# Two 32-head attentions on one core: unread matrix products in slots short of work, and a reordered start and end

## The chip, the cores and the metric

The kernel runs on one core of a Trainium2 chip. The metric is the device time of one execution in microseconds (us), smaller is better; it is the median of several executions. The engines are TensorE (PE in the profile, its weight loads PEld), VectorE (DVE), ScalarE (ACT), GpSimd (POOL) and SyncE (SP). They run at the same time, each through its own queue in order, and wait for each other by semaphores.

## The reference

Two attention blocks of the same shape, A over all keys and B over a sliding window, are computed from separate inputs and laid side by side in the output. x is 2048 x 512, wqkv 512 x 1536, wo 512 x 512, all bf16.

```python
def attention(x, wqkv, wo, window=None):        # B=1, S=2048, D=512, H=32, Dh=16
    q, k, v = split_heads(x @ wqkv)
    scores = einsum("bhqd,bhkd->bhqk", q, k) * Dh ** -0.5
    if window:                                  # block B: window = 256
        d = idx[:, None] - idx[None, :]
        scores = where((d >= 0) & (d < window), scores, -1e9)
    p = softmax(scores, axis=-1)
    return merge_heads(einsum("bhqk,bhkd->bhqd", p, v)) @ wo
out = concatenate([attention(A_x, A_wqkv, A_wo), attention(B_x, B_wqkv, B_wo, 256)], -1)
```

The great mass of the work is the exponential: for A alone 32 x 2048 x 2048 elements. With heads only 16 wide the matrix products have little to multiply per element of the scores.

## The kernel before

**Units, jobs, slots.** A unit is one block, one pass of 512 queries and one group of four heads. Its jobs are score tiles of 128 keys by 512 queries for one head. Three jobs make a slot (`SLOT = 3`): one PSUM tile `sps` of three banks, of which there are two. `slots` (L796) writes all jobs into one list of 755 slots, with B's units spread between A's. The four heads of a group use row groups 32j of the array, so that their score products run beside each other (L517); the products of probabilities and values use column groups 32j in the same way (L621).

**One turn of the loop.** `run` (L905) writes out the order of every engine's queue by hand. For slot s it issues the exponential of slot s on ScalarE (`exps`, L544), perhaps one step of a vector-side exponential (`dq`), the score products of slot s+2 (`scores`), the value products whose probabilities are ready (`values`), the transfers and small steps that are due (`later`), and then as many filling steps as a credit allows (`fill`, L889). Since there are two `sps` tiles, the scores of slot s+2 wait until the exponential of slot s has read its tile.

**Filling steps.** Projections of q, k and v, output products, and the score products of the jobs whose exponential VectorE computes as a polynomial (L571 to L595) are tasks with a due slot (`plan`, L819). Most are pairs: the first step opens PSUM bank `ms` (there is one) and does half the products, the second does the other half and empties the bank. While a pair is open, `self.open` holds the bank. `queued` and `freed` keep an estimate of when VectorE will have emptied it, in units of `PITCH` = 1.345 us a slot.

**The filler that is there.** In `scores`, where fewer than two steps were filled in the slot before and the job is A's, a product of 128 rows and 512 columns (L512) goes into the same `sps` bank first; the real score product then overwrites it.

**Sums and division.** Values carry a column of ones, so that each unit's bank `op` (one) also gets the softmax denominators. `epilogue` copies `op` to `osb` (L675) and sends it through DRAM; the denominators are gathered, inverted, spread and multiplied in four later steps (L681 to L703). Only the last two units of A's last pass divide in place (`end`, L641): a reciprocal of the whole bank (L649), ScalarE's copy (L651), four fp32 products that spread the reciprocals over rows (L655), and one multiply (L658). `last_out` (L402) then makes A's last output tile from five products for each of four query chunks and writes it out.

**Start.** `start` (L709) turns the tokens of A chunk by chunk (`turn`), copies them to SBUF (`keep`), makes the keys of the first two head groups with padding (`keys`, L443), the first queries, two value tiles, and the guard row that keeps exponents in range (`pad_guard`: L465, L467, L470, L472). `more_constants` sets up masks and fills eight DRAM scratch tensors `kd` and `qd` by GpSimd's queue.

Of the kernel before, what the change touches and what calls it, by code (L numbers as in the profile page):

```python
# [14 lines left out]
P = 128  # L15
H = 32
# [87 lines left out]
class _Kernel:  # L104

    def __init__(self, ctx, tc, tensors, out):
        self.tc, self.nc = tc, tc.nc
        self.t = tensors
        self.out = out
        pool = lambda name, **kw: ctx.enter_context(tc.tile_pool(name=name, **kw))  # L110
        self.consts = pool("consts", bufs=1)
        self.sb = pool("sb", bufs=1)
        self.ps = pool("ps", bufs=1, space=bass.MemoryType.PSUM)
        self.dram = pool("dram", bufs=1, space=bass.MemoryType.DRAM)
        self.xT, self.w, self.wo, self.kT, self.v, self.qT = {}, {}, {}, {}, {}, {}
        self.acol, self.negas, self.oT = {}, {}, {}
        self.op, self.od = {}, {}
        self.later = []
        self.slot = self.ended = self.closed = -1
        self.pend, self.guards, self.dq = [], [], []  # L120
        self.open = None
        self.filled = 2
        self.vec = self.freed = 0.0
        self.last_poly = -1
# [6 lines left out]

    def queued(self, us, bank=False):

        self.vec = max(self.vec, self.slot * PITCH) + us
        if bank:
            self.freed = self.vec


    def constants(self):
# [5 lines left out]
        pick(self.ident[:], self.ident[:], pattern=[[1, P]], compare_op=ALU.is_equal,  # L145
             fill=0.0, base=0, channel_multiplier=-1)
        self.wpad = self.tile([P, 2, NC, 2, P], BF16, "wo", 2)
        nc.gpsimd.memset(self.wpad[:].bitcast(FP32), 0.0)
# [169 lines left out]
    def v_evac(self, i, t, bank, copy, h=(0, H)):  # L318
        if i == 1:
            self.v_begin(i, t)  # L320
        v3 = self.v[i, t][:, 0:H * VP].rearrange("p (h d) -> p h d", d=VP)
        self.queued(OP, True)
        copy(out=v3[:, h[0]:h[1], 1:VP],
             in_=bank[:, 0:(h[1] - h[0]) * DH].rearrange("p (h d) -> p h d", d=DH))
# [77 lines left out]
    def last_out(self, i, p):  # L402

        nc = self.nc
        o, wo = self.oT[i, p], self.wo[i]
        big = [self.ps.tile([P, SLOT, 512], FP32, name="sps", tag="sps", bufs=2)
               for _ in range(2)]
        banks = [big[qc % 2][:, qc // 2, :] for qc in range(4)]

        def mm(qc, c):  # L410
            w = wo[:, c, :] if c < NC - 1 else self.wend[:, c - NC + 1, :]
            nc.tensor.matmul(banks[qc], lhsT=o[c][:, qc * P:(qc + 1) * P], rhs=w,  # L412
                             start=(c == 0), stop=(c == NC))
        for qc in range(4):
            for c in range(NC):
                mm(qc, c)

        def finish():
            obs = self.tile([P, SLOT, 512], BF16, "pT", 6)
            for qc in range(4):  # L420
                mm(qc, NC)
            for qc in range(4):
                ob = obs[:, qc, :] if qc < SLOT else self.tile([P, D], BF16, "ob", 2)[:]
                (nc.scalar.copy if qc % 2 else nc.vector.tensor_copy)(out=ob, in_=banks[qc])
                q0 = p * 512 + qc * P
                (nc.scalar if qc % 2 else nc.sync).dma_start(
                    self.out[q0:q0 + P, i * D:(i + 1) * D], ob)
        return finish

# [72 lines left out]
    def scores(self, slot):  # L502
        sps = self.ps.tile([P, SLOT, 512], FP32, name="sps", tag="sps", bufs=2)
        for b, jb in enumerate(slot["jobs"]):
# [4 lines left out]
            if b == 0 and self.filled < 2 and jb.inst == 0:  # L509

                kT, k0 = self.kT[jb.inst, jb.g // 2, jb.subs[0][0] // 4]
                self.nc.tensor.matmul(sps[:, 0, 0:WARM], lhsT=kT[:, gg, k0:k0 + P],  # L512
                                      rhs=qT[:, gg, 0:WARM], start=True, stop=True)
# [89 lines left out]
    def values(self):  # L603


        while self.pend:
# [4 lines left out]
            if key not in self.op:  # L611
                if self.ended >= self.slot - 1:
                    return
                self.op[key] = self.ps.tile([P, 512], FP32, name="op", tag="op", bufs=1)
                self.started = set()
            op = self.op[key]
            self.pend.pop(0)
            for jb in group:
                h = 4 * jb.g + jb.j
# [21 lines left out]
    def end(self, i, p, g):  # L641


        nc = self.nc
        op = self.op[i, p, g]
        ones = self.tile([P, 32], FP32, "den", 2)
        nc.gpsimd.memset(ones[:], 1.0)
        rec = self.tile([P, 512], FP32, "oc", 2)
        nc.vector.reciprocal(out=rec[:], in_=op[:])  # L649
        osb = self.tile([P, 512], FP32, "osb", 2)  # L650
        nc.scalar.copy(out=osb[:], in_=op[:])  # L651
        b = self.bank()
        for j in range(GH):
            r = slice(32 * j, 32 * j + 1)
            nc.tensor.matmul(b[32 * j:32 * j + 32, :], lhsT=ones[r, :], rhs=rec[r, :],  # L655
                             start=True, stop=True, tile_position=(32 * j, 32 * j))
        o = self.tile([P, 512], BF16, "oTa", 5)
        nc.vector.tensor_mul(out=o[:], in0=osb[:], in1=b[:])  # L658
        self.closed = self.slot
        self.queued(2.2, True)  # L660
        self.oT.setdefault((i, p), []).append(o)

    def epilogue(self, i, p, g):
# [11 lines left out]
        nc.vector.tensor_copy(out=osb[:], in_=self.op[i, p, g][:])  # L675
        self.queued(OP)
        nc.sync.dma_start(od[g % 2], osb[:])
        if g % 2 == 0:
# [11 lines left out]
        def invert():  # L690
            den = st["den"]
            nc.vector.reciprocal(out=den[:], in_=den[:])
            self.queued(0.35)
            st["rd"] = self.dram.tile([8, 512], FP32, name="rd", tag="rd", bufs=3)
# [6 lines left out]
        def scale():  # L701
            o = self.tile([P, 512], BF16, "oT" + n, 5)
            nc.vector.tensor_mul(out=o[:], in0=st["oc"][:], in1=st["rb"][:])  # L703
            self.queued(OP)
            self.oT.setdefault((i, p), []).append(o)
# [3 lines left out]
    def start(self):  # L709
# [28 lines left out]

        def busy(n):

            b = self.bank()
            for _ in range(n):
                nc.tensor.matmul(b[:, 0:P], lhsT=self.ident[:], rhs=self.ident[:],
                                 start=True, stop=True)

        def turn(c):
# [17 lines left out]
        def keys(c):  # L764
            b = tile_("op", 1) if c % 2 == 0 else self.bank()
            self.pad_mm(1, 0, c, b[:], range(NC))
            self.pad_k_evac(0, c, b[:])
        for t in range(NKT):
            self.v_begin(0, t)
        busy(36)  # L770
        turn(0)
        keep(0)
        turn(1)
        keys(0)
        keep(1)
        b = self.bank()
        self.pad_mm(0, 0, 0, b[:], range(NC))
        mq = self.pad_q_evac(0, b[:])
        for c in range(2, NPASS):
            turn(c)  # L780
            keys(c - 1)
            keep(c)
        keys(NPASS - 1)
        nv = 2
        for t in range(nv):
            vb = tile_("op", 1)
            self.v_mm(0, t, vb[:], range(NC), (0, HV))
            self.v_evac(0, t, vb[:], nc.scalar.copy, (0, HV))
            if t == 0:
                self.pad_guard(0, mq)  # L790
                self.qT[0, 0, 0] = self.padq
        self.more_constants()
        self.load_wo(0)
        return [("v", 0, t, 0) for t in range(nv)] + [("k", 0, 0), ("q", 0, 0, 0)]
# [24 lines left out]
    def plan(self, slots, done):  # L819
# [24 lines left out]
        for t in range(NKT):  # L844
            task(("v", 0, t, 0), vneed[0, t] - 1, self.v_steps(0, t, (0, HV)))
            task(("v", 0, t, 1), begin[0, 0, 2] - 16 + t, self.v_steps(0, t, (HV, H)),
                 [("v", 0, t, 0)])
# [41 lines left out]
    def fill(self, s, tasks, done):  # L889

        if self.open is None:
            if self.closed == s or self.freed > (s + 0.5) * PITCH:
                return False
# [11 lines left out]
    def run(self):  # L905
        done = set(self.start())
        self.vec = self.freed = 0.0
        slots, self.pend = self.slots()
# [4 lines left out]
        for s, sl in enumerate(slots):  # L913
            self.slot = s
            self.exps(sl)
            if self.dq and self.vec <= (s + 0.4) * PITCH:
                self.queued(1.22)
                self.dq.pop(0)()
            if s + 2 < len(slots):
                self.scores(slots[s + 2])  # L920
            self.values()
            due = [x for x in self.later if x[0] <= s]
# [10 lines left out]
            if (self.guards and self.guards[0][0] <= s and self.open is None  # L933
                    and self.freed <= (s + 0.5) * PITCH):
                self.guards.pop(0)[1]()
                self.closed = s
            while credit >= 1.0 and self.fill(s, tasks, done):
                credit -= 1.0
                self.filled += 1
        finish = self.last_out(0, NPASS - 1)  # L940
        while self.pend:
# [55 lines left out]
```

## Time and profile before

| | |
|---|---|
| time, median of three | 1124.56 us (1121.5 to 1127.27) |
| span of the profiled execution | 1120.5 us |
| ScalarE busy | 1033.3 us, 92% |
| TensorE busy | 974.3 us, 87% |
| VectorE busy | 636.4 us, 57% |
| GpSimd busy | 20.4 us, 2% |
| mean granted TensorE clock | 0.927 |
| chain that ended last | ACT 48%, PE 34%, issue 10%, DVE 7% |

The busy share of TensorE is that of its instructions' durations, which get longer when its clock is lowered; a busy TensorE is therefore not one at its peak. The clock line of the page gives the granted share of the full clock in tenths for each fortieth of the span (28 us). The chain is followed back from the last instruction to what released each one, and says which engine held up the end.

### The profile page before, as it was taken

The page shows a single profiled execution, that of the slowest core. Times are in us where ns is not written, and L with a number is a line of the kernel's source. Part 1 is how long each engine was busy: PE and PEld are TensorE (multiplying, and loading weights), DVE is VectorE, ACT ScalarE, POOL GpSimd, SP SyncE. Part 2 cuts the span into 40 slices and gives each one's busy share as a digit, 9 for nine tenths or more (in the row PEclk, how much of TensorE's full clock was granted, in tenths as well). Part 3 has the DMA queues.
Part 4 walks back from the last instruction along what each step waited for, and adds up shares of the span by engine and source line. Part 5 has one row for each costly group of instructions (what it writes and reads, how often), then busy time and mean ns, then how long its engine had stood idle before and what let it go on. Part 6 is the DMA issues. An engine that isn't in the chain of part 4 may idle for free.

```text
span 1120.5 us, 18311 instructions
## 1 busy us (share of the span) xinstructions
PE 974.3 (87%) x7463; PEld 310.7 (28%) x7463; DVE 636.4 (57%) x843; ACT 1033.3 (92%) x787; POOL 20.4 (2%) x101
## 2 busy tenths in 40 slices
PE   5898888888889898998898889988789988889986
PEld 3232222232223223222322233323223222322211
DVE  3353221115877668774588756768476782874532
ACT  3799999999999999999999999999999999998974
POOL 6000000000000000000000000000000000000000
PEclk8899999889999989898999999989988998986568
DMA  7021331122412114120221321113012121200100
GB/s 227 1 82 58 109 101 43 39 72 73 127 60 75 42 42 130 46 68 31 66 88 63 92 69 63 58 59 111 20 43 70 54 77 40 78 30 1 59 5 33
DMA packets 72356, 73.01 MB, mean 65 GB/s; under 512 B 22584, under 2 KB 55888, under 8 KB 72272
## 3 DMA queue, kind: packets, MB, share of 16 engines
q1 hardware_dynamic: 69072, 67.88, 20.2%
q10 hardware_dynamic: 2432, 1.84, 0.5%
q0 software_dynamic: 768, 2.13, 0.5%
q8 instruction: 58, 0.95, 0.4%
q14 instruction: 26, 0.21, 0.1%
HBM read 38.65 MB, written 31.07 MB: 62 GB/s over the span
## 4 chain that ended last, share of the span: by engine, by line
ACT 48%; PE 34%; issue 10%; DVE 7%; DMA 1%; ACTq 0%; SPq 0%; DVEq 0%
ACT pT L544 47%; PE sps L517 8%; PE op L621 7%; PE ms L230 6%; PE sps L512 6%; PE sps L526 3%; PE ms L571 2%; DVE dy L574 1%; DVE dh L585 1%; DVE oc L649 1%; PE sps L412 1%; DVE qs L350 0%; DVE gs L364 0%; DVE osb L675 0%; DVE pD L595 0%
## 5 line engine op out<-in xcount | busy, mean ns | idle before, releaser
L544 ACT ACTIVATE pT<-sps 128x1536 bf16<-128x1536 f32 (+2 forms) x771 | 1022.6, 1475 | 50.2 <-PE sps L517 34.5
L512 PE MATMUL sps<-qTa,kTa 128*128 128x512 bf16 x570 | 233.2, 409 | 91.8 <-ACT pT L544 88.6
L517 PE MATMUL sps<-qTa,kTa 32*128 32x512 bf16 x1880 | 269.9, 413 | 1.5 <-ACT pT L544 1.1
L621 PE MATMUL op<-pT,va 128*32 128x512 bf16 x1880 | 200.9, 419 | 0.6 <-ACT pT L544 0.6
L574 DVE COPY dy<-ms 128x512 f32<-128x512 f32 x168 | 115.3, 686 | 130.9 <-PE ms L571 129.1
L517 PEld LDWEIGHTS <-kTa 32*128 32x128 bf16 x1880 | 63.1, 92 | 306.8 <-issue 306.8
L585 DVE SCALAR_TENSOR_TENSOR dh<-dy 128x1024 f32<-128x1024 uint16 x84 | 102.4, 1219 | 1.7
L595 DVE SCALAR_TENSOR_TENSOR pD<-dh,dy 128x1024 uint16<-128x1024 f32 x84 | 102.2, 1217 | 1.2
L589 DVE SCALAR_TENSOR_TENSOR dh<-dy,dh 128x1024 f32<-128x1024 uint16 x84 | 102.0, 1214 | 1.0
L512 PEld LDWEIGHTS <-kTa 128*128 128x128 bf16 x570 | 55.8, 98 | 146.4 <-issue 132.4
L621 PEld LDWEIGHTS <-va 128*32 128x32 bf16 x2048 | 50.9, 95 | 118.7 <-issue 116.5
L526 PE MATMUL sps<-mask,ident 128*128 128x128 bf16 (+1 forms) x640 | 79.3, 251 | 0.0
L571 PE MATMUL ms<-qTa,kTa 32*128 32x512 bf16 x168 | 67.6, 402 | 6.8 <-DVE gs L364 2.1
L517 PE MATMUL sps<-qTb,kTb 32*128 32x384 bf16 (+2 forms) x704 | 60.9, 278 | 8.9 <-ACT pT L544 8.5
L675 DVE COPY osb<-op 128x512 f32<-128x512 f32 x62 | 42.7, 688 | 45.3 <-PE op L621 44.9
L248 DVE CAST kst<-ms 128x512 bf16<-128x512 f32 x28 | 19.3, 690 | 67.4 <-PE ms L230 67.1
L350 DVE TENSOR_SCALAR qs<-ms 128x512 bf16<-128x512 f32 x31 | 21.2, 685 | 62.2 <-PE ms L230 61.0
L526 PEld LDWEIGHTS <-ident 128*128 128x128 bf16 x640 | 44.0, 98 | 33.7 <-issue 30.8
L395 DVE CAST ob<-ms 128x512 bf16<-128x512 f32 x28 | 19.3, 688 | 42.9 <-PE ms L230 42.7
L230 PE MATMUL ms<-wv,xT 128*128 128x512 bf16 (+2 forms) x184 | 38.0, 321 | 4.5 <-DVE dy L574 2.9
L230 PE MATMUL ms<-xT,wq 128*128 128x512 bf16 x124 | 38.2, 409 | 0.4 <-DVE dy L574 0.2
L621 PE MATMUL op<-pT,vb 128*32 128x384 bf16 (+2 forms) x704 | 36.3, 280 | 0.0
(98 smaller groups left out, 411.4 us busy)
## 6 DMA issues: line engine op xcount, KB each, us to landing
od<-osb SPq DMA_DIRECT2D x62, 256.0 KB
oc<-od SPq DMA_DIRECT2D x31, 256.0 KB
rb<-rd SPq DMA_DIRECT2D x31, 256.0 KB
kTb<-kd SPq DMA_DIRECT2D x16, 256.0 KB
qTb<-qd SPq DMA_DIRECT2D x16, 256.0 KB
qd<-qs SPq DMA_DIRECT2D x31, 128.0 KB
qTa<-qd SPq DMA_DIRECT2D x15, 256.0 KB
kd<-kst SPq DMA_DIRECT2D x28, 128.0 KB
```

Of the source, the lines that this page charges most:

```text
L230: self.nc.tensor.matmul(bank, lhsT=lhs(c), rhs=rhs(c), start=(c == 0), stop=(c == NC - 1))
L512: self.nc.tensor.matmul(sps[:, 0, 0:WARM], lhsT=kT[:, gg, k0:k0 + P], rhs=qT[:, gg, 0:WARM], start=True, stop=True)
L517: self.nc.tensor.matmul(sps[:, b, o:o + q1 - q0], lhsT=kT[r, gg, k0:k0 + P], rhs=qT[r, gg, q0:q1], start=(o == jb.subs[0][3]), stop=not jb ...
L526: self.nc.tensor.matmul(sps[:, b, o:o + P * len(kind)], lhsT=self.ident[:], rhs=m, start=False, stop=True, skip_group_check=True)
L544: nc.scalar.activation(out=pT[:, b:e, :n], in_=sps[:, b:e, :n], func=ACT.Exp, scale=LN2 / 128, bias=-127 * LN2)
L571: nc.tensor.matmul(b[:], lhsT=kT[r, g % 2, k0:k0 + P], rhs=self.qT[0, p, g // 2][r, g % 2, :], start=True, stop=True, tile_position=(32 * ...
L574: nc.vector.tensor_copy(out=y[:, half, :], in_=b[:])
L585: nc.vector.scalar_tensor_tensor(out=st["h"][:], in0=low, scalar=-65536.0, in1=low, op0=ALU.add, op1=ALU.mult)
L589: nc.vector.scalar_tensor_tensor(out=st["h"][:], in0=low, scalar=65536.0 * POLY[1], in1=st["h"][:], op0=ALU.add, op1=ALU.mult)
L595: nc.vector.scalar_tensor_tensor(out=out.bitcast(U16), in0=st["h"][:], scalar=POLY[0] * 2.0 ** -41, in1=flat, op0=ALU.mult, op1=ALU.add)
L621: self.nc.tensor.matmul(op[32 * jb.j:32 * jb.j + 32, q0:q1], lhsT=self.v[jb.inst, kt][:, h * VP:h * VP + 32], rhs=jb.pT[:, o:o + q1 - q0], ...
L675: nc.vector.tensor_copy(out=osb[:], in_=self.op[i, p, g][:])
```

## The change

Four things are changed. (1) A slot short of work on TensorE gets one or two products of the identity with itself, 512 columns each, into bank `ms`; nobody reads them (`busy`). `self.work` adds up an estimate of TensorE's work in a slot for this. They are to keep TensorE evenly occupied. (2) The estimates of VectorE's queue are made later by 0.7 of a slot for work that follows TensorE (`at`), the tests against them are loosened to match (`by`), the next unit may take `op` as soon as it is estimated free (`op_free`), and the second part of the value tiles is due later. (3) In `end` VectorE makes the copy of the bank for the first of the two units, and for the last one the output products that don't need it (`first`) are issued beside the reciprocal (`mid`); the spread and the multiply go in two halves of 256 columns. (4) At the start the tokens are kept before the keys are made, four value tiles instead of two are made there, seven unread products stand around the guard, all value tiles' ones are set at once, and the masks and DRAM scratch follow in slot 2.

```diff
+    def queued(self, us, bank=False, at=0.7):
+        self.vec = max(self.vec, (self.slot + at) * PITCH) + us
...
+    def by(self, t, at):
+        return t <= (self.slot + at) * PITCH
+
+    def busy(self, n):
+        b = self.bank()
+        for _ in range(n):
+            self.nc.tensor.matmul(b[:], lhsT=self.ident[:], rhs=self.junk, start=True,
+                                  stop=True)
...
+        self.junk = self.ident[:].unsqueeze(1).broadcast_to((P, 4, P))
...
-                if self.ended >= self.slot - 1:
+                if self.ended == self.slot or not self.by(self.op_free, 0.5):
                     return
...
-        nc.scalar.copy(out=osb[:], in_=op[:])
+        (nc.scalar.copy if self.mid else nc.vector.tensor_copy)(out=osb[:], in_=op[:])
+        if self.mid:
+            self.mid()
+        o = self.tile([P, 512], BF16, "oTa", 5)
         b = self.bank()
-        for j in range(GH):
...
-        nc.vector.tensor_mul(out=o[:], in0=osb[:], in1=b[:])
+        for q in (slice(0, 256), slice(256, 512)):
+            for j in range(GH):
+                r = slice(32 * j, 32 * j + 1)
+                nc.tensor.matmul(b[32 * j:32 * j + 32, q], lhsT=ones[r, :], rhs=rec[r, q],
+                                 start=True, stop=True, tile_position=(32 * j, 32 * j))
+            nc.vector.tensor_mul(out=o[:, q], in0=osb[:, q], in1=b[:, q])
         self.closed = self.slot
-        self.queued(2.2, True)
+        self.queued(5.0, True)
+        self.op_free = self.vec
...
         turn(1)
+        keep(1)
         keys(0)
-        keep(1)
...
             turn(c)
+            keep(c)
             keys(c - 1)
-            keep(c)
         keys(NPASS - 1)
-        nv = 2
+        nv = 4
...
+        self.busy(3)
+        self.pad_guard(0, mq)
+        self.busy(4)
+        self.qT[0, 0, 0] = self.padq
-        self.more_constants()
-        self.load_wo(0)
...
-            task(("v", 0, t, 1), begin[0, 0, 2] - 16 + t, self.v_steps(0, t, (HV, H)),
+            task(("v", 0, t, 1), begin[0, 0, 2] - 4 + t, self.v_steps(0, t, (HV, H)),
...
-            if self.closed == s or self.freed > (s + 0.5) * PITCH:
+            if self.closed == s or not self.by(self.freed, 0.9):
...
+            if s == 2:
+                self.more_constants()
+                self.load_wo(0)
...
+            self.work = 0.33
             if s + 2 < len(slots):
                 self.scores(slots[s + 2])
+            elif s + 1 == len(slots):
+                self.mid, finish = self.last_out(0, NPASS - 1)
...
                 self.filled += 1
+                self.work += 0.4
+            if self.work < 0.8 and self.open is None and self.by(self.freed, 0.9):
+                self.closed = s
+                self.busy(2 if self.work < 0.6 else 1)
-        finish = self.last_out(0, NPASS - 1)
```

The work estimate also takes 0.22 for the L512 product and 0.33 for each group of value products.

## The prediction

> **What bounds the kernel now.** I read the page first, then the busy time of each engine in chosen stretches, then the chain of waits at the start, at the two places with a full-width reciprocal, and at the end, and last the list of waits.
>
> ```profile
> ACT  3799999999999999999999999999999999998974
> PEclk8899999889999989898999999989988998986568
> L544 ACT ACTIVATE pT<-sps 128x1536 bf16<-128x1536 f32 (+2 forms) x771 | 1022.6, 1475 | 50.2 <-PE sps L517 34.5
> L512 PE MATMUL sps<-qTa,kTa 128*128 128x512 bf16 x570 | 233.2, 409 | 91.8 <-ACT pT L544 88.6
> ```
>
> The reader is to see that ScalarE is busy nearly throughout with the exponentials of L544, that it still stands idle for 50.2 us before them, most of it until a score product (L517) is done, and that the TensorE clock dips again and again, worst in slices 36 to 39. The page gives a mean clock of 0.927; the trace knows only 1.0 and 0.5, so 0.073/0.5 = 15% of 1120.5 us, 166 us, ran at half clock. The same stretches by engine:
>
> ```profile
> core 0: us, PE busy (x) PEld busy (x) DVE busy (x) ACT busy (x) POOL busy (x), PEclk, DMA share, GB/s
> 128.00:141.40 13.40, 10.03 (x76) 2.85 (x76) 1.38 (x2) 13.40 (x11) 0.00 (x0) 1.00 0.54 137
> 212.60:216.00 3.40, 2.19 (x20) 0.69 (x17) 0.00 (x0) 3.40 (x4) 0.00 (x0) 1.00 0.39 93
> 216.10:222.80 6.70, 6.70 (x31) 1.33 (x30) 1.64 (x3) 5.39 (x4) 0.00 (x0) 0.50 0.13 41
> 1014.80:1035.20 20.40, 20.40 (x107) 4.65 (x106) 9.55 (x11) 15.69 (x12) 0.00 (x0) 0.50 0.00 1
> ```
>
> At full clock (first row) ScalarE is busy without a gap and TensorE has air. Just before a drop (second row) TensorE has less work than elsewhere. At half clock (third and fourth rows) TensorE is busy 100% and ScalarE waits: 12 exponentials in 20.4 us, 1.70 us each, where the undisturbed spacing of their starts is 1.33 us. So the kernel is bound by ScalarE, except where the slowed TensorE takes over. Laying the starts of all 771 exponentials in the trace side by side, the 89 gaps that lie mostly at half clock add up to 164.4 us, 46.0 us more than 1.33 us per full exponential (the short ones of the window attention counted by their length); the other 681 gaps lose 35.8 us. Of the 46.0 us, 5.7 belong to one gap of 7.02 us that is no clock matter (below), which leaves 40.3 us for the 14 drops inside the loop and the one just before it, 2.7 us each.
>
> ```profile
> 1070.81 3.37 DVE oc L649
> 1074.18 0.02 issue
> 1074.20 0.58 ACT osb L651
> 1074.79 2.71 ACT pT L544 x2
> ...
> 1103.76 3.37 DVE oc L649
> 1107.12 0.14 issue
> 1107.26 1.93 PE ms L655 x8
> 1109.19 6.70 PE sps L412 x20
> ```
>
> Here the chain of waits shows the in-place division: reciprocal, then ScalarE's copy of the same bank, and only then the next exponential; and after the last exponential (ends 1103.28) 17.2 us of tail, of which 6.70 are the output product at half clock.
>
> ```profile
> 18.81 1.04 PE ms L230 x4
> ...
> 21.58 1.79 DVE padneg L467
> ...
> 25.52 2.80 ACT pT L544 x2
> ```
>
> The start is a chain of turned tokens, keys and the guard; the first exponential begins at 25.52 us. From the list of waits (who waited for whom: us in total, times, longest):
>
> ```profile
> ACT osb L651 <- DVE oc L649: 9.0, 2, 5.1
> PE ms L230 <- DVE dy L574: 5.6, 12, 0.9
> ```
>
> The first is the division again; the second is nearly all that TensorE now waits for bank ms.
>
> [...] only 0.5 and 1.0 occur, and all changes stand on a grid of 3.41 us. [...] here the clock falls with TensorE at work in two thirds of a window. [...] L651 waits 9.0 us in two calls for L649, both readers of op. [...] in the trace the pairs of 512-column products at full clock stand 0.22 us apart, at half clock 0.43.
>
> **What makes the clock fall.** For each 3.41 us window I summed columns/clock of the products, weighted by the share of the array's rows and columns that they use (a slot's three score products together 3/4, the 32-row products of the vector-side exponentials 1/4). Thirteen of the 14 drops in the loop follow a window of 0.34 to 0.385, one of 0.25; of all windows that kept full clock six are under 0.37. The way back takes a window of about 0.75 or more at half clock. A usual slot of 1.335 us has the filler product L512 (0.213), scores (0.213 x 3/4 = 0.16), values (0.213): 0.59/1.335 = 0.44. Every fourth slot has no values: 0.37/1.335 = 0.28. A window over one such bare slot comes to about (0.37 + 1.56 x 0.59)/3.41 = 0.38, just at the edge.
>
> **The change part by part.**
> (1) Unread products. Counted from the order of both programs, 115 of 752 slots of the old one have neither values nor filled work; in the new one 36, because 96 slots get unread products (69 two, 27 one, 165 in all). A bare slot with two has 0.37 + 0.43 = 0.80 us, and its window 0.50. Stretches of three slots with less than 1.55 us of weighted work fall from 47 to 12. What stays is where a pair of projection steps is held open over several slots (the bank is taken), and the four slots after the first division. 14 drops for 47 stretches makes 3 to 4 for 12; I take 4 at 2.7 us = 10.8, so 40.3 - 10.8 = 29.5 us are gained. The cost: 165 x 0.22 = 36 us of TensorE, which lies in slots that use 0.64 us of 1.335, beside the exponential. Behind an unread product in TensorE's queue stand the next slot's scores, and ScalarE waits for those; the product itself waits for VectorE to empty bank ms. Such waits are now 5.6 us for dy, 3.0 for padmax and 2.1 for gs in all, and the new due times put VectorE later, on the careful side. Cost between 0 and 36 us; I take 1.5.
> (2) Estimated VectorE times, later values of heads 9 up, an op bank reused one slot earlier: slots with two steps fall from 57 to 46, those with one rise from 325 to 345. Two steps add 0.85 us to a slot and overrun by about 0.3: 11 x 0.3 = 3, less 20 x 0.08: 2 us gained.
> (3) First division: VectorE copies instead of ScalarE. The gap of 7.02 us becomes a usual one, 5.7 gained; values then stand still for four slots and come back three groups at once (4 x 0.33 us), 0.7 lost: 5 us.
> (4) Tail from the last exponential: 17.2 us now. New: 0.5 values, 3.36 reciprocal with the 16 first products beside it (16 x 0.22 = 3.5, at full clock [...]), a half of the spread and its multiply 0.5 + 0.4, the other half 0.5 + 0.4, last products and casts 1.5, then 2.9 from last cast to end as now: 10.1. Gain 7 us; at half clock the 16 take 6.9 us and the gain is 3.5.
> (5) Start. Copying tokens before keys takes two waits of ScalarE (0.7 us each) off the token loop; TensorE then has 8.3 us of products from 7.90 on and about 1 us of waits, so the last keys end near 17.2 instead of 19.85: 2.6. padneg took 1.78 us beside GpSimd's memsets of vb and 0.25 without (the two calls of L467); the memsets now come earlier: 1.5 gained. Two more value tiles are hidden in the guard's wait, but the four unread products behind the guard wait until VectorE has read bank ms and stand ahead of the first scores: 4 x 0.22 = 0.9 lost. 3 us gained. The scratch transfers have no reader until the first k_evac, far later: nothing.
>
> Sum: 29.5 - 1.5 + 2 + 5 + 7 + 3 = 45. 1124.56 - 45 = **1080 us**.
>
> **The rivals.**
> (B) The drops stay where the bank is held, or one drop still lasts long as at 1042 to 1069: half of the 40.3 us remains. For it: the 36 bare slots, and a bound of 0.37 that a window of plain slots clears by little. Against: the stretches fall by three quarters. 1124.6 - 20 - 15 + 4 = 1094 (the 15 from parts 3 to 5, the 4 for a dearer filler).
> (C) No drop is left, and fewer double slots pay in full. For it: the two long half-clock stretches from 1015 to 1069 us (10 of the 40.3 us) lie where the new program has fillers. Against: four stretches with under 1.45 us remain. 1124.6 - 40.3 - 15 - 3 = 1066.
> (D) Slower: each filled slot stalls on bank ms for a whole VectorE step (0.7 us, the dy copy), 96 x 0.7 = 67 us more, against 45: 1147. [...] Against: TensorE now meets such a wait some twenty times in the whole run, though 381 of the old slots carry a step into that bank.
>
> **Chances.** My forecast 0.62, B 0.17, C 0.17, D 0.04. The range goes from C's 1066 less 4 us for the median's own scatter to B's 1094 and 4 us more: 1062 to 1098, with D and the worse half of B left out. Faster by over 0.5% (under 1119): all but D and a little of B, 0.94; within 0.5%: 0.02; slower: 0.04.
>
> **What would show it.** The clock line should show mostly 9s with three to five dips, the mean 0.96 to 0.98; ScalarE's idle time before the exponentials should fall from 50 us to about 30; the chain should show no ScalarE copy near 1030 us; the last reciprocal should have 16 output products beside it; the first exponential should begin near 22.5 us. I am wrong if the clock still dips in ten slices or more, if TensorE waits long on bank ms, or if the tail keeps 17 us.

## The result and the profile after

The kernel after the change takes 1097.2 us (median; 1092.48 to 1099.26), the kernel before beside it 1125.91 (1121.5 to 1133.16): a ratio of 0.9733, 95% interval 0.967 to 0.9796. A second comparison of the same pair, with more executions (below), gives 1093.44 against 1127.72 and 0.9695 (0.9658 to 0.9733). So 29 to 34 us are gained; 45 were forecast, and 1080 us. Medians here and below are over all executions, while the ratios leave out the few in a slower state (one of 1151.08 us shows a mean clock of 0.742); without these the 1124.43 us below would be 1123.39, and the 1100.69 us 1098.81.

From the page of the kernel after, the busy share of ScalarE and the clock in 40 slices, the groups of the exponential and of the score filler, which are now L559 and L527, and the group of the unread products:

```profile
ACT  5899999999999999999999899999998999999976
PEclk9999999999999999999999899999996999997989
L559 ACT ACTIVATE pT<-sps 128x1536 bf16<-128x1536 f32 (+2 forms) x771 | 1020.8, 1484 | 46.0 <-PE sps L532 29.7
L527 PE MATMUL sps<-qTa,kTa 128*128 128x512 bf16 x580 | 227.4, 392 | 70.6 <-ACT pT L559 62.6
L146 PE MATMUL ms<-ident 128*128 128x512 bf16 x172 | 53.7, 382 | 9.7 <-DVE dy L589 2.2
```

The clock line has four slices below 9 (23, 31, 37 and 39), where the kernel before had 16; the mean is 0.970 instead of 0.927. The unread products hardly wait for their bank: 9.7 us for 172, of which 2.2 for the dy copies. But ScalarE still stands idle for 46.0 us before its exponentials, not for about 30.

The four stretches of the prediction, from the timeline of the kernel after (start, duration, engine, line, what; in brackets the idle time before it and what ended that). First the first division:

```profile
1053.52 3.36 DVE L665 RECIPROCAL oc<-op 128x512 f32<-128x512 f32 x1
1056.79 0.63 DVE L667 COPY osb<-op 128x512 f32<-128x512 f32 x1
...
1057.02 0.63 PE L675 MATMUL ms<-oc,den 1*32 1x256 f32 x8 [3.55 <-DVE oc L665]
...
1058.19 1.07 PE L675 MATMUL ms<-oc,den 1*32 1x256 f32 x8 [0.53 <-DVE oTa L677]
...
1059.19 0.61 PE L527 MATMUL sps<-qTa,kTa 128*128 128x512 bf16 x1
...
1060.45 2.79 ACT L559 ACTIVATE pT<-sps 128x1536 bf16<-128x1536 f32 x2 [5.44 <-PE sps L532]
```

ScalarE copies nothing here any more, and yet it is idle for 5.44 us. The gap between two starts of the exponential is 7.17 us; before it was 7.02. TensorE waits 3.55 us for the reciprocal with the first spread product (L675), and the next scores, begun by L527, stand behind it and behind the second half of the spread (L527 starts at 1059.19).

The tail:

```profile
1086.67 0.82 PE L425 MATMUL sps<-wo,oTa 128*128 128x512 bf16 x2
1086.78 3.36 DVE L665 RECIPROCAL oc<-op 128x512 f32<-128x512 f32 x1 [1.74 <-PE op L637]
...
1090.28 0.64 PE L675 MATMUL ms<-oc,den 1*32 1x256 f32 x8
1091.04 0.42 DVE L677 TENSOR_TENSOR oTa<-osb,ms 128x256 bf16<-128x256 f32 x1 [0.91 <-PE ms L675]
...
1092.22 0.42 DVE L677 TENSOR_TENSOR oTa<-osb,ms 128x256 bf16<-128x256 f32 x1 [0.76 <-PE ms L675]
...
1094.54 0.36 ACTq L440 DMA_DIRECT2D out_dram<-ob  x1
```

The sixteen output products lie beside the reciprocal at full clock (1086.67 to 1090.3). From the end of the last exponential (1086.3) to the end of the span (1097.55) it is 11.25 us instead of 17.24.

And the start:

```profile
18.23 0.25 DVE L481 TENSOR_SCALAR padneg<-padsel,amax 128x128 bf16<-128x128 bf16 x1
...
21.09 1.02 PE L146 MATMUL ms<-ident 128*128 128x512 bf16 x4 [0.84 <-DVE qTa L486]
...
22.48 2.79 ACT L559 ACTIVATE pT<-sps 128x1536 bf16<-128x1536 f32 x2 [2.99 <-PE sps L532]
```

The guard's padneg takes 0.25 us (1.79 before), the four unread products behind the guard stand ahead of the first scores for about 1.0 us (0.9 forecast), and the first exponential starts at 22.48 instead of 25.52.

**Where the time went.** Laid side by side as in the prediction (each exponential's start-to-start time less 1.33 us for a full one, sorted by the clock in it, the gap of the division apart), the two profiled executions of the kernel after give, in us gained over the kernel before:

```
                                        forecast   first profile   second profile
start                                      3.0          3.0             3.2
tail                                       7            6.0             5.8
loss at half clock (was 40.3)             29.5         22.7            30.9
loss at full clock (was 35.8)              0.5         -8.6            -9.9
gap of the first division (was 7.02)       5           -0.1            -0.4
sum                                       45           23.0            29.6
span                                                   23.0            29.7
```

The 0.5 is the forecast's 2 us of part 2 less its 1.5 us for the unread products; both would be seen in that row. The rows add up by the way they are made; what they show is where the gain lies. Two rows carry a shortfall in both executions: the division, and the loss at full clock. Half clock varies: 68.6 us of the first execution ran at it, 47.3 of the second, of the same program, and only in the first does that row fall short as well (by 6.8 us).

### The profile page after: what moved, and what is told of

The parts are those of the page before. It is cut to its first block, busy times and chain, and to the rows that moved or that the text cites. A ratio compares the mean times of both kernels' runs of the same rounds, so it can differ in the third digit from the quotient of the medians.

```text
span 1097.5 us, 18628 instructions
## 1 busy us (share of the span) xinstructions
PE 973.1 (89%) x7583; PEld 322.0 (29%) x7661; DVE 636.7 (58%) x844; ACT 1031.8 (94%) x788; POOL 20.3 (2%) x101
## 4 chain that ended last, share of the span: by engine, by line
ACT 50%; PE 29%; issue 11%; DVE 8%; DMA 1%; SPq 0%; ACTq 0%; DVEq 0%
ACT pT L559 50%; PE sps L532 6%; PE op L637 6%; PE ms L242 6%; PE sps L527 4%; PE sps L541 4%; DVE dy L589 2%; PE ms L586 2%; PE ms L146 1%; DMA kTa<-in_A_x_dram 1%; DVE dh L600 1%; DVE pD L610 1%; DVE gs L376 0%; DVE qs L362 0%; DVE ob L407 0%
## 5 line engine op out<-in xcount | busy, mean ns | idle before, releaser
L559 ACT ACTIVATE pT<-sps 128x1536 bf16<-128x1536 f32 (+2 forms) x771 | 1020.8, 1484 | 46.0 <-PE sps L532 29.7
L527 PE MATMUL sps<-qTa,kTa 128*128 128x512 bf16 x580 | 227.4, 392 | 70.6 <-ACT pT L559 62.6
L532 PE MATMUL sps<-qTa,kTa 32*128 32x512 bf16 x1880 | 259.7, 397 | 1.5 <-ACT pT L559 1.3
L637 PE MATMUL op<-pT,va 128*32 128x512 bf16 x1880 | 193.4, 402 | 0.3 <-DVE osb L695 0.2
L532 PEld LDWEIGHTS <-kTa 32*128 32x128 bf16 x1880 | 62.9, 91 | 289.5 <-issue 289.1
L527 PEld LDWEIGHTS <-kTa 128*128 128x128 bf16 x580 | 56.4, 97 | 130.3 <-issue 108.2
L541 PE MATMUL sps<-mask,ident 128*128 128x128 bf16 (+1 forms) x640 | 78.7, 249 | 0.0
L532 PE MATMUL sps<-qTb,kTb 32*128 32x384 bf16 (+2 forms) x704 | 59.8, 276 | 3.4 <-ACT pT L559 1.7
L146 PE MATMUL ms<-ident 128*128 128x512 bf16 x172 | 53.7, 382 | 9.7 <-DVE dy L589 2.2
L541 PEld LDWEIGHTS <-ident 128*128 128x128 bf16 x640 | 43.7, 98 | 32.7 <-issue 30.0
L242 PE MATMUL ms<-wv,xT 128*128 128x368 bf16 (+2 forms) x171 | 37.4, 315 | 2.9 <-DVE padmax L462 0.8
```

Source lines behind the costliest of these rows:

```text
L146: self.nc.tensor.matmul(b[:], lhsT=self.ident[:], rhs=self.junk, start=True, stop=True)
L242: self.nc.tensor.matmul(bank, lhsT=lhs(c), rhs=rhs(c), start=(c == 0), stop=(c == NC - 1))
L532: self.nc.tensor.matmul(sps[:, b, o:o + q1 - q0], lhsT=kT[r, gg, k0:k0 + P], rhs=qT[r, gg, q0:q1], start=(o == jb.subs[0][3]), stop=not jb ...
L541: self.nc.tensor.matmul(sps[:, b, o:o + P * len(kind)], lhsT=self.ident[:], rhs=m, start=False, stop=True, skip_group_check=True)
L559: nc.scalar.activation(out=pT[:, b:e, :n], in_=sps[:, b:e, :n], func=ACT.Exp, scale=LN2 / 128, bias=-127 * LN2)
L637: self.nc.tensor.matmul(op[32 * jb.j:32 * jb.j + 32, q0:q1], lhsT=self.v[jb.inst, kt][:, h * VP:h * VP + 32], rhs=jb.pT[:, o:o + q1 - q0], ...
```

## The experiments

All times stand against the kernel before, run beside them.

**Without the unread products of the loop.** The three that stand in the start's guard and the four behind it stay.

```diff
-            if self.work < 0.8 and self.open is None and self.by(self.freed, 0.9):
-                self.closed = s
-                self.busy(2 if self.work < 0.6 else 1)
```

> The changed kernel without the unread products in the loop (the seven around the guard at the start stay; nothing that is read is left out). Theory 1 (the products keep the clock up, at little cost): the clock drops some 12 to 15 times in the loop again, mean clock near 0.93 as before, 15 to 25 us slower than the changed kernel: about 1115 us. Rival (the gain came from the reordered fills and VectorE estimates): clock and time stay within 5 us of the changed kernel, 1097 us.

Measured: 1124.43 us, ratio 0.9962 (0.9934 to 0.9991). Its page:

```profile
PEclk9999999999999799986996999999889986756859
L559 ACT ACTIVATE pT<-sps 128x1536 bf16<-128x1536 f32 (+2 forms) x771 | 1023.7, 1476 | 68.3 <-PE sps L532 41.8
```

The clock dips about as often as before (13 slices below 9, before 16) but for longer (206 us at half clock, before 166), and ScalarE's idle time rises to 68.3 us. Start and tail give their 9 us in this trace too (first exponential 22.32, tail 11.24), but the half-clock loss is 49.5 us, 9 more than before. So the new order without the products costs much of what the start and tail bring: the ratio's interval leaves 1 to 7 of the 9 us.

Why it loses more at half clock is open. It isn't the number of bare slots. The rule gives two products where the program's estimate of the work is under 0.6 and one where it is not, so the 27 slots with a single one already hold values or a step. Without the products the new order has at most 36 + 69 = 105 bare slots, where the prediction counted 115 in the old one. The lists of waits only say where ScalarE waits longer: for the scores of L532 41.8 us (34.5 before, at L517), and for B's masked scores of L541 24.4 us (13.1 before, at L526).

**The unread products on the old order.** The kernel before, with `busy` and the loop's rule alone, and the bank's old limit.

```diff
+    def busy(self, n):
...
+                self.work += 0.22
...
+            self.work += 0.33
...
+            self.work = 0.33
...
+                self.work += 0.4
+            if (self.work < 0.8 and self.open is None
+                    and self.freed <= (s + 0.5) * PITCH):
+                self.closed = s
+                self.busy(2 if self.work < 0.6 else 1)
```

> The kernel before with the loop's unread products alone, under its own estimates of VectorE. Theory 1: most of the clock's part of the gain without the start's 3 and the tail's 6 us: 15 to 20 us faster than before, about 1107 us, clock 0.96 to 0.975. Rival (the products cost about as much in crowded slots as they save, and the rest of the change pays): within 6 us of before, 1120 to 1126 us. The loss of exponential starts at full clock, 36 us before and 44 us in the changed kernel, should rise to about 44 here if the products are its cause, and stay at 36 if the reordering is.

Measured: 1100.32 us, ratio 0.978 (0.9738 to 0.9821). In its profiled execution, the fastest of six at 1096.78 us, the half-clock loss is 5.9 us, the full-clock loss 45.9, the clock 0.981. The products alone take 34.4 us of half-clock loss away and give 10.1 back at full clock. They are most of the whole gain, about 27 of 29 to 34 us, and a full-clock loss of about 45 us comes with them, in either order of the program.

**The unread products on 32 rows.** The same products in the same slots, but with a quarter of the array's rows.

```diff
-    def busy(self, n):
+    def busy(self, n, rows=P):
...
+            if rows < P:
+                self.nc.tensor.matmul(b[:], lhsT=self.ident[0:rows, :],
+                                      rhs=self.junk[0:rows], start=True, stop=True,
+                                      tile_position=(0, 0))
+                continue
...
-                self.busy(2 if self.work < 0.6 else 1)
+                self.busy(2 if self.work < 0.6 else 1, 32)
```

> The changed kernel with the loop's unread products on 32 rows of the array in place of 128: same count, same 512 columns, same place in the queue. Theory 1 (what counts is columns times the share of the array in use): the drops come back as without the products, mean clock 0.93 to 0.94, about 1115 us. Rival (TensorE only has to be busy, however few rows work): as the changed kernel, clock 0.97 to 0.98, 1097 us.

Measured: 1102.67 us, ratio 0.9762 (0.9703 to 0.9821). Its page:

```profile
PEclk9999999999999999999999789999898999999759
L147 PE MATMUL ms<-ident 32*128 32x512 bf16 x165 | 53.0, 388 | 9.1 <-DVE dy L594 2.5
```

The 165 products last as long as the full ones (388 ns each in the page's measure, against 382) and hold the clock at 0.962, nearly as well as with 128 rows (0.970 and 0.979). A weight by the share of rows, which the prediction used, would have made them worth a quarter. The half-clock loss is 22.1 us here, 17.6 and 9.4 in the two profiles of the kernel after, and 49.5 without the products. The interval overlaps that of the kernel after, so a small part of the effect may hang on the rows; a quarter doesn't fit.

**The first division's spread four slots later.** Reciprocal and copy stay where they are; spread products and multiply go into the list of guards.

```diff
+        self.queued(4.05)
+        self.op_free = self.vec
+
+        def spread():
...
         if self.mid:
             self.mid()
...
+            spread()
+        else:
+            self.guards.append((self.slot + 4, spread))
```

> The changed kernel with the first division's spread products and multiply issued four slots later, when the reciprocal is done. Theory 1 (TensorE stands in order behind the reciprocal, so that the next scores wait for it whoever copies the bank): the gap of 7.2 us between two exponentials near 1053 us shrinks to under 2 us, and 4 to 6 us are gained: about 1092 us. Rival (the gap is VectorE's or the op bank's): the gap stays over 5 us, 1097 us.

Measured: 1093.26 us, ratio 0.9713 (0.9674 to 0.9751). From its timeline, the same place:

```profile
1052.98 3.36 DVE L665 RECIPROCAL oc<-op 128x512 f32<-128x512 f32 x1
1053.18 0.38 PE L527 MATMUL sps<-qTa,kTa 128*128 128x512 bf16 x1 [0.25 <-ACT pT L559]
...
1053.81 0.61 PE L146 MATMUL ms<-ident 128*128 128x512 bf16 x2
...
1056.26 0.63 DVE L667 COPY osb<-op 128x512 f32<-128x512 f32 x1
...
1058.60 0.63 PE L677 MATMUL ms<-oc,den 1*32 1x256 f32 x8
```

Scores and unread products run on while VectorE divides, ScalarE has no gap there (12 exponentials in 16.40 us from 1043.45 on), and the spread finds its reciprocal ready. The 7 us gap is gone; the largest left near it is 2.84 us. In the kernel after, then, the wait is the order of TensorE's queue, not the copy, which stands where it stood. Deferring the spread with ScalarE's copy left in place is not tested; in the kernel before, ScalarE stood for 5.09 us behind the same reciprocal with that copy, so a wait would likely have stayed.

The time of this run alone doesn't show the gain: its ratio lies between the two of the kernel after (0.9733 and 0.9695), and its profile has 16.2 us of half-clock loss, against 9.4 in the second profile of the kernel after. A pair of runs below shows the gain.

**Part 2 undone.** The estimates, limits, op bank and due times of the kernel before in the kernel after.

```diff
-    def queued(self, us, bank=False, at=0.7):
+    def queued(self, us, bank=False, at=0.0):
...
-                if self.ended == self.slot or not self.by(self.op_free, 0.5):
+                if self.ended >= self.slot - 1 or not self.by(self.op_free, 0.5):
...
-        self.op_free = self.vec
...
-            if self.closed == s or not self.by(self.freed, 0.9):
+            if self.closed == s or not self.by(self.freed, 0.5):
...
-            task(("v", 0, t, 1), begin[0, 0, 2] - 4 + t, ...)
+            task(("v", 0, t, 1), begin[0, 0, 2] - 16 + t, ...)
```

> The changed kernel with its part 2 undone: VectorE estimates, the 0.5 limit for a free bank, the op bank two slots after a group's end and the due times of the later value halves as in the kernel before; unread products, division, start and tail stay as changed. Theory 1 (the new order itself lowers the clock more often and only the unread products hide it: the run without unread products gained 2.7 us where its start and tail alone give 9): with the old order the half-clock loss falls from 17.6 us towards the 5.9 of the run that added only the unread products, so 1086 to 1092 us. Theory 2 (the new order pays the 2 us that the prediction gave it, or is neutral): 1096 to 1100 us.

Measured: 1091.39 us, ratio 0.9702 (0.9663 to 0.9741). The time is the one that theory 1 expected, but it has to be laid beside a second measurement of the kernel after. Three more runs give that, and two pieces of part 2 apart. **Only the due times undone** (the last hunk alone):

> The changed kernel with only the due times of the later value halves (heads 9 up) back at 16 slots ahead. Theory 1 (this bunching of tasks is what part 2 costs): 1086 to 1092 us like the run with all of part 2 undone. Theory 2 (the cost sits in the estimates and the limit of 0.9, which let products into more slots but move other work): within 3 us of the changed kernel, 1094 to 1100.

Measured: 1100.69 us, ratio 0.9785 (0.9743 to 0.9826). **Only the estimates and limits undone** (`queued` and the limit 0.9 alone, the latter at all three places where it is tested):

> The changed kernel with only the VectorE estimates and the limit for a free bank back as in the kernel before; the op bank one slot after a group's end and the later due times stay as changed. Theory 1 (these estimates are what part 2 costs): as the run with all of part 2 undone, ratio 0.969 to 0.972. Theory 2 (the cost is spread over the pieces or lies in the op bank's earlier reuse): as the changed kernel, 0.973 to 0.977.

Measured: 1092.26 us, ratio 0.9698 (0.9659 to 0.9737). **The kernel after once more**, with no edit:

> The changed kernel once more, beside the other two on one chip, so that part 2 can be weighed with more rounds. Theory 1 (part 2 costs 4 to 5 us): ratio 0.973 to 0.976, above the 0.9702 of the run with part 2 undone. Theory 2 (part 2 is neutral): 0.969 to 0.972.

Measured: 1093.44 us, ratio 0.9695 (0.9658 to 0.9733). That is what the kernel with part 2 undone has (0.9702), and theory 2 of this last run holds: with the unread products in place, part 2 as a whole gains or costs nothing that these runs can tell. The first profile of the kernel after (17.6 us of half-clock loss) was one with many drops; the second has 9.4. The theory that the new order costs 4 to 5 us falls. A cost of it is seen only in the run without the unread products. Whether the later due times help once the estimates are changed (0.9785 without them, 0.9733 and 0.9695 with them) is left open.

**Part 2 undone and the spread deferred.** Both edits shown above in one kernel.

> As the run with the old order, and the first division's spread products and multiply issued four slots later, out of the way of the scores. Theory 1: both gains add up, 4 to 6 us under that run, so 1081 to 1087 us, the fastest so far. Theory 2 (the wait merely moves to another place once the drops are few): the same as that run within 2 us.

Measured: 1084.58 us, ratio 0.9658 (0.9618 to 0.9698), 6.8 us under the run with part 2 undone, on the same chip: both gains add up, as theory 1 has it. The intervals of the two overlap, but five of the six executions lie below all six of that run. What is left of the half-clock loss (9.6 us) has one long stretch; the stretches before and in it, from the view of engines by window:

```profile
core 0: us, PE busy (x) PEld busy (x) DVE busy (x) ACT busy (x) POOL busy (x), PEclk, DMA share, GB/s
990.00:993.30 3.30, 2.88 (x22) 0.76 (x22) 2.27 (x2) 3.30 (x3) 0.00 (x0) 1.00 0.00 0
993.30:996.70 3.40, 2.35 (x21) 0.63 (x17) 0.69 (x1) 3.40 (x4) 0.00 (x0) 1.00 0.02 5
996.70:1003.00 6.30, 6.30 (x30) 1.14 (x29) 2.92 (x3) 5.39 (x5) 0.00 (x0) 0.50 0.00 0
```

The stretch ahead of the drop, 69% busy, holds slots of score filler, scores and values and one 32-row product. They count 0.88 us by the program's estimate and get no unread product, as the limit is 0.8.

**Twice as many unread products in the same slots.**

```diff
-                self.busy(2 if self.work < 0.6 else 1)
+                self.busy(4 if self.work < 0.6 else 2)
```

> The changed kernel with twice as many unread products in the same slots (four or two in place of two or one, 165 more). Theory 1 (in a slot that is short of work a product is hidden and costs about 0.03 us; what is left of the drops lies where no product is allowed): 165 x 0.03 = 5 us more at full clock and perhaps a drop less, 1095 to 1103 us. Theory 2 (TensorE is the bound in such slots, each product at its full 0.22 us): 36 us more, about 1133. Theory 3 (the products that stand there are too few to hold the clock): the half-clock loss of 17.6 us falls by half, about 1088.

Measured: 1111.33 us, ratio 0.9884 (0.9846 to 0.9923). None of the three theories: the clock is high (0.988), the half-clock loss 6.3 us, but the full-clock loss rises to 64.3 us without the division's gap. Beside the second profile of the kernel after (45.7) that is 18.6 us for 165 products, 0.11 us each. The timeline of this run shows one way in which they cost:

```profile
957.54 0.34 PE L541 MATMUL sps<-mask,ident 128*128 128x256 bf16 x2
...
957.70 0.68 DVE L589 COPY dy<-ms 128x512 f32<-128x512 f32 x1
...
958.43 1.02 PE L146 MATMUL ms<-ident 128*128 128x512 bf16 x4 [0.55 <-DVE dy L589]
...
959.39 0.40 PE L532 MATMUL sps<-qTb,kTb 32*128 32x128 bf16 x6
959.72 0.67 PE L541 MATMUL sps<-mask,ident 128*128 128x256 bf16 x6
...
960.49 1.45 ACT L559 ACTIVATE pT<-sps 128x1536 bf16<-128x1536 f32 x1 [0.95 <-PE sps L541]
```

The four products wait 0.55 us until VectorE has emptied bank `ms`, run for 1.02 us, and only then come B's scores with their masks; ScalarE stands for 0.95 us. The products lie ahead of scores that are needed next. Over the whole run it is not the bank that costs. ScalarE's waits for B's masked scores, from the list of waits of the kernel after and then of this run, and the group of the unread products in this run:

```profile
ACT pT L559 <- PE sps L541: 13.2, 34, 0.7
...
ACT pT L559 <- PE sps L541: 22.5, 59, 1.4
...
L146 PE MATMUL ms<-ident 128*128 128x512 bf16 x337 | 89.0, 379 | 10.5 <-DVE dy L589 2.7
```

The waits before the unread products come to 10.5 us, against 9.7 with half as many. The waits for B's scores grow by 9.3 us (10.6 beside the second profile of the kernel after, 11.9), about half of the 18.6. Where the rest lies is open.

**One product more where there was none.** The kernel of the run with part 2 undone and the spread deferred, with the limit raised so that slots with values take one product too (119 more).

```diff
-            if self.work < 0.8 and self.open is None and self.by(self.freed, 0.5):
+            if self.work < 0.9 and self.open is None and self.by(self.freed, 0.5):
```

> The run with the old order and the deferred spread, and one unread product also in slots whose only work besides the scores are the values (limit 0.9 in place of 0.8; 119 more products, all in slots that have 0.88 us of work by the program's count). Theory 1 (the drops that are left, 9.6 us of half-clock loss, begin in windows of such slots, and a product there is nearly free, 0.05 us each): 9.6 us less 2 to 3 that stay, plus 6, so 1080 to 1085 us, no worse than that run. Theory 2 (the price rises with what the slot already holds, to the 0.12 us each that the doubled products showed or more): 119 x 0.12 = 14 us more against 7 less, 1090 us or above.

Measured: 1082.92 us (1082.26 to 1084.1), ratio 0.96 (0.9567 to 0.9633), the fastest of all, ahead of both the kernel before and the one after. Its page:

```profile
PEclk9999999999999999999999999999999999999999
L559 ACT ACTIVATE pT<-sps 128x1536 bf16<-128x1536 f32 (+2 forms) x771 | 1019.4, 1485 | 30.3 <-PE sps L532 16.7
L146 PE MATMUL ms<-ident 128*128 128x512 bf16 x292 | 100.0, 384 | 12.7 <-DVE dy L589 4.6
```

The mean clock is 0.995; 14.4 us at half clock remain, half of them in the tail, and 3.4 us of loss in the loop. The full-clock loss is 47.4 us against 46.1 without the 119 products, over some 15 more slots: they cost nothing that these profiles show. Theory 1 holds. The step from 1084.58 to 1082.92 us itself is not clear of noise, as the intervals of the two ratios overlap; the half-clock loss, 3.4 us in the loop against 9.6, is what shows the effect. The idle time before the exponentials is now the 30 us that the prediction gave the kernel after.

## Why the prediction was right, and where its sum was off

The sign and the range hold (1062 to 1098); the point, 1080, is 13 to 17 us too low.

- **Mechanism.** Right as to the unread products, which keep the clock up. The run without them (1124.43 us, mean clock 0.909 in its profile), the run with them alone (1100.32, 0.981) and the run with 119 more (1082.92, 0.995) show it. That it is bare slots that let the clock fall was the author's estimate from the windows of the kernel before. The count of what stays was near: a half-clock loss of 10.8 us was forecast, 17.6 and 9.4 were found.
- **Step (1), its cost.** Mis-sized: 1.5 us, with the 2 us that part 2 should bring back. The full-clock loss rose by 8.6 and 9.9 us. Part of this is the yardstick: a slot at full clock doesn't take 1.33 us but loses 0.053 of its own (35.8 us over 681 slots before), so that the 53 to 65 slots which moved from half to full clock bring only the difference: 2.8 to 3.4 us. The rest, about 6 us, is a loss of 0.061 a slot in place of 0.053. It comes with the unread products in the old order as well (0.061); without them the new order has 0.057. So half of it or more is theirs, some 0.02 to 0.04 us for each of 165. The 0.22 us a product in the sums is what the trace of the kernel before shows: products of 512 columns that follow each other in the tail (L412) start 0.216 us apart at full clock and 0.427 at half, in the median.
- **Step (1), its measure.** The weight by rows is refuted for these products by the run with 32 rows. The forecast survived it by luck, since the products of the change use all rows. The edge of 0.37 was worked out with that weight, and with 0.213 us for 512 columns, which is half of the 0.427 above, and doesn't stand without the weight; the measure that would take its place is open.
- **Step (2).** 2 us forecast; nothing that can be measured with the unread products, and 9 us more of half-clock loss without them. The prediction worked with the count of double and single slots and put no cost of the new order on the clock; what in the order causes it stays open, since its bare slots are not more.
- **Step (3).** Wrong: 5 us forecast, none found. It took the chain's piece of ScalarE's copy for the wait. It was one of two that lay on each other, as the timeline and the list of waits of the kernel before show:

```profile
1074.20 0.58 ACT L651 COPY osb<-op 128x512 f32<-128x512 f32 x1 [5.09 <-DVE oc L649]
1074.31 1.93 PE L655 MATMUL ms<-oc,den 1*32 1x512 f32 x8 [3.56 <-DVE oc L649]
...
1076.19 0.59 PE L512 MATMUL sps<-qTa,kTa 128*128 128x512 bf16 x1
...
PE ms L655 <- DVE oc L649: 7.1, 2, 3.6
```

TensorE stood behind the same reciprocal with the spread products, and the next scores (L512) after those. This wait was in the list too, 7.1 us in two. (Nor are the 5.6 us for dy nearly all of TensorE's waits for bank `ms`, as the prediction has it under the list: the 3.0 and 2.1 us that its step (1) names come to almost as much.) The kernel after shows the same order (L527 starts at 1059.19, behind the spread products that start at 1058.19), and the deferred spread gives the gain that was missing: 6.8 us in one pair of runs.

- **Steps (4) and (5).** Nearly right: the tail takes 11.3 to 11.5 us (forecast 10.1) and gains 5.8 to 6.0 of the 7 us, the first exponential starts at 22.48 (22.5).
- **Rivals.** B's time, 1094, is nearest. Its reason, half of the 40.3 us left, fits the first profile (17.6) but not the second (9.4), where the drops went as forecast. C's 1066, with no drop left, was not reached even by the run at a clock of 0.995 (1082.92). D's stalls on bank `ms` didn't come: 9.7 us of waits before 172 products.

## What to carry to other kernels

Filling a TensorE that is short of work can be worth far more than the filler costs (34.4 us of half-clock loss against 10.1 at full clock, on the old order), but spread it thinly. One product in each of 119 further slots cost nothing that could be seen, while doubling those of 96 slots cost 0.11 us for each added one, about half of it in B's scores, which stand behind them. The two were tried on different orders of the program, so the number in a slot isn't quite parted from the rest. When a wait is taken from the critical path, look in every other queue for an instruction that waits for the same producer; here the same reciprocal held TensorE just as long. And measure the slow phase against what a good slot really takes, not against the shortest one.

## What the runs showed of the hardware

The clock mostly fell with TensorE at work. In the kernel before, TensorE was busy for 2.17 to 2.66 of the 3.41 us ahead of twelve of the loop's 14 drops; in the kernel after, for 2.27 to 2.36 ahead of the drops at 621.3, 658.9, 822.7 and 1003.6; and in the run with part 2 undone and the spread deferred, for 2.35 of the 3.40 us ahead of its long one. What exactly is weighed stays open. In the loops of these two kernels only the drop at the first division goes with a pause of more than 3.41 us (3.55 us idle in the kernel after, half clock from 1058.2; 3.56 in the kernel before, from 1072.8). Unread products of 32 rows keep the clock nearly as those of 128 do (0.962 against 0.970 and 0.979). Score products of one slot run beside each other, and value products too: at full clock three, on 32 rows each, take 0.39 us together and four value products 0.40, where one filler product on the whole array takes 0.38 (kernel before, from 1099.72). And the same program lost 17.6 us to half clock in one execution and 9.4 in another; no run here tells why. The kernel with hardly any drop also has the narrowest times: 1082.26 to 1084.1 us over six executions, against 1091.6 to 1096.26 for the kernel after on the same chip.
